# Attention and two feed-forward layers on one core: a planner's waits, row stores, read bursts, output copies and load depth

## The chip, the cores and the metric

The kernel runs on one NeuronCore of a Trainium2 chip, in one launch. The metric is device time in microseconds (us), lower is better. Five engines work side by side, each through its own instructions in order: TensorE (PE in the profile, with its weight loads as PEld), VectorE (DVE), ScalarE (ACT), GpSimd (POOL) and SyncE (SP), which issues every DMA here. They meet only in semaphores.

## The reference

Attention of 4 batches, 12 heads, 448 positions and 64 channels, with an RMS norm on queries and keys, followed by two feed-forward layers on the 1792 x 768 result:

```python
q_n, k_n = (rmsnorm(q, g_q), rmsnorm(k, g_k))
scores = scale * np.matmul(q_n, k_n.transpose(0, 1, 3, 2))
attn = softmax(scores)                       # over the last axis
x = np.matmul(attn, v)                       # to (B*S, H*D) = (1792, 768)
h = x @ w_in;  x = np.maximum(h, 0.0) ** 2 @ w_out          # d_ff 2048
g = x @ w_gate;  x = (silu(g) * (x @ w_val)) @ w_out        # d_ff 1536
```

## The kernel before, in words

**Pairs of heads.** Attention works on 24 pairs of heads, six pairs to a batch. For a pair, `all_scores` writes four groups of score tiles to PSUM (sc), `softmax` takes their maxima on VectorE and the exponentials on ScalarE into a ring of six tiles (ring), `all_transposes` turns each of the seven tiles on TensorE into a PSUM bank (pt), `turned_tile` copies it out, mostly on ScalarE, and `all_values` multiplies by v into another PSUM bank (o). `pair_outputs` multiplies o by the inverse sums (zb), which gives the rows ox; `finished_rows` stores ox to DRAM (x1d) and splits it in two parts, a rounded one and the rest, as x1. Two PSUM banks (`t_banks`) serve pt, o, small transposes (rows) and, for the first pairs, spread vectors.

**Spread vectors.** Key scales (rk) and inverse sums (zb) are needed along the other axis. For the first five pairs TensorE spreads them; from pair 5 (`SPREAD_K`, `SPREAD_Z`) they go to DRAM and are read back, broadcast, in two pieces (rkb, L646) and three pieces (zb, L808). For pairs below `SPREAD_Z` the o bank is copied out first, and is free at once; for the others it is held until zb has come.

**Fillers.** While attention runs, TensorE fills its spare time with the first six column blocks of the first layer for batches 0 to 2 (`ffn1a`: h_a and ya) and the beginning of batch 3 (`lead`: h_lead, lead2). They need the x1 of a whole batch and decoded weights.

**Sweeps.** Then `products` runs 14 sweeps: a sweep takes one batch over some column blocks f, with h products (or h_g and h_v) of 18 matmuls each, and 18 matmuls into the six PSUM banks y0 to y5 two blocks later (`BEHIND`). While a sweep runs, `load_x` fetches the six tiles xr of the next one from DRAM, casts each on ScalarE (L214) and subtracts on VectorE (L1101). `Partial` fetches earlier partial sums (yp), and `written` takes y out of PSUM and stores it. Six SBUF tiles (`io_free`) are shared by xr, yp and the copies of y. All matmuls use two-part operands, so a product takes three passes (`mm3`). The weights come in 8-byte words (raw) and are decoded by ScalarE, VectorE and GpSimd (wa, wt, hi, lo).

**Who sets the order.** The program is written by a planner in Python. Every piece of work is a generator that yields the costs of its next instruction on the engines that could run it (`{"A": 467, "V": 535}`, ns), a condition, or a number, which is a wait in planned time. `simulate` runs a clock over them; `dispatch` gives a free engine the job of the lowest rank and emits the instruction. A planned wait emits nothing: it only changes what is emitted before what. Attention has rank by pair, fillers come last. SP's jobs cost 475 ns each, and a transfer is taken to land 900 ns after its share of 300 bytes per ns.

Of the kernel before, what the change touches and what calls it, by code (L numbers as in the profile page):

```python
# [10 lines left out]
F32R = mybir.dt.float32r  # L11
# [6 lines left out]
B, H, S, D = 4, 12, 448, 64  # L18
# [33 lines left out]
BEHIND = 2  # L52
X_AT = 3
DEC_FIRST = 14
DEC_STEP = 6
# [4 lines left out]
PREP_AHEAD = 4  # L60
DMA_MARGIN = 0
A_SPARE = 600
# [12 lines left out]
def attention_two_ffn_kernel(  # L75
# [141 lines left out]

    def dma(issue, nbytes):
        yield DMA_MARGIN
        while nbytes >= DMA_BULK and dma_free[0] > clock[0] + 1100 + DMA_QUEUE:  # L220
            yield dma_free[0] - clock[0] - 1100 - DMA_QUEUE
        yield {"S": 475}, issue, nbytes

# [283 lines left out]
    def stats(b, p, n):  # L507
# [18 lines left out]
        if b * PB + p + n > SPREAD_K:  # L526
            yield from dma(lambda e: e.dma_start(out=rk_d[b][p * PT:(p + n) * PT, :], in_=rows), 0)
        rkr_free.append(where)
# [110 lines left out]
    def load_rk(g, kr):  # L639
        b, p = divmod(g, PB)  # L640
        yield lambda: rk_free and g in rows_ready
        where = rk_free.pop(0)
        rk = tile_at(where, [128, S], F32, f"rkb{g}")
        for i in range(2):
            yield from dma(
                lambda e: e.dma_start(out=rk[64 * i:64 * i + 64], in_=half(rk_d[b], 2 * p + i, 64)), 64 * S * 4  # L646
            )
        yield from prep_k(g, kr, rk, where)
# [51 lines left out]
    def probs(n):  # L700

        return ring[:, n % RING]

    def all_scores(me):
        for n in range(NH // 2 * len(GROUPS)):
# [4 lines left out]
            yield lambda: s_banks and g in qs and g in ks  # L710
            where = s_banks.pop(0)
            bank = tile_at(where, [128, 2, 512], F32, f"sc{n}")
            parts = [bank[:, t] for t in range(2)]
# [65 lines left out]
    def norms(g):  # L779
# [19 lines left out]
        yield 200  # L799
        yield from dma(lambda e: e.dma_start(out=z_d[g], in_=rows), 0)  # L800
        zr_free.append(zr_at)
# [3 lines left out]
        flat = z_d[g].rearrange("r c -> (r c)")  # L805
        for p, to, at, w in ((0, 0, 0, S), (64, 384, S, 64), (64, 0, 512, 384)):
            src = flat[bass.ds(at, w)].unsqueeze(0).to_broadcast([64, w])
            yield from dma(lambda e: e.dma_start(out=zb[p:p + 64, to:to + w], in_=src), 64 * w * 4)  # L808
        zinv[g] = zb, zb_at

    def all_transposes(me):


        for n in range(NT):
# [7 lines left out]
            ps = tile_at(where, [128, 512], F32, f"pt{n}")  # L822
            p = probs(n)

            def turn(e):
# [21 lines left out]
    def all_values(me):  # L847
        for g in range(NH // 2):
# [4 lines left out]
            o = tile_at(o_at, [128, S], F32, f"o{g}")  # L853
            v, v_at = vs.pop(g)

            def chain(e):
# [12 lines left out]
    def pair_outputs(g, o, o_at):  # L869

        yield settle["P"]
        yield lambda: ox_free and (g < SPREAD_Z or g in zinv)
        ox_at = ox_free.pop(0)
        ox = tile_at(ox_at, [128, S], F32, f"ox{g}")
        if g < SPREAD_Z:
            yield {"A": 467, "V": 535}, lambda e: copy(e, ox, o)
            t_banks.append(o_at)
            o = ox
            yield lambda: g in zinv
        zb, zb_at = zinv.pop(g)  # L880
        yield {"V": 535}, lambda e: e.tensor_tensor(out=ox, in0=o, in1=zb, op=ALU.mult)
        if g >= SPREAD_Z:
            t_banks.append(o_at)
        (zb_free if zb_at[0] is ap else t_banks).append(zb_at)
        yield from finished_rows(g, ox, ox_at)

    def finished_rows(g, ox, ox_at):
# [9 lines left out]
        def store():  # L897
            yield from dma(lambda e: e.dma_start(out=x1_d[b][j], in_=ox), 128 * S * 4)
            let_go()
# [186 lines left out]
    def x_tiles(n, second, ts):  # L1086
        def tile_of(j):
            pool = xp2 if second and j < 4 else xp
            ts.append(pool.tile([128, 2, S], F32R, tag=f"x{j + 2 if second and j >= 4 else j}", name=f"x_{n}_{j}"))
            return ts[j]  # L1090

        return tile_of

    def load_x(src, n, tiles, done):

# [11 lines left out]
        for j in range(KD):  # L1107
            yield lambda: io_free
            yield from part(j, io_free.pop(0))

# [6 lines left out]
    def products():  # L1117
# [4 lines left out]
        for i, (layer, b, fs, last_use, partial, dst) in enumerate(sweeps):  # L1122
            n = f"{layer}_{i}"
            done = None
            for f in fs:
                if f == fs[X_AT if len(fs) > 6 else 1] and i + 1 < len(sweeps):
                    nxt, done = [], []
                    src = (x1_d if sweeps[i + 1][0] == 1 else x2_d)[sweeps[i + 1][1]]
                    spawn(load_x(src, n, x_tiles(n, i % 2 == 0, nxt), done), k)
                name = f"{n}_{f}"  # L1130
# [30 lines left out]
    class Partial:  # L1161
# [6 lines left out]
        def load(self):  # L1168
            while io_free and len(self.tiles) < KD:
                j = len(self.tiles)  # L1170
                self.at[j] = io_free.pop(0)
# [19 lines left out]
    def out_of(name, n, layer, f, first, last, release_it, ys, sums, dst, k):  # L1191
# [3 lines left out]
        s, where = ready.pop(name)  # L1195
        for j in range(KD):
            if first:
                ys[j] = ps_y.tile([128, S], F32, tag=f"y{j}", name=f"y_{n}_{j}")
            yield from mm3(ys[j], w[0], w[1], bass.ts(j, 128), s[:, 0, :], s[:, 1, :], first, last)
            if last:  # L1200
                spawn(written(ys[j], sums, j, n, dst[j]), k - 2)
# [87 lines left out]
```

## Time and profile before

| | us |
|---|---|
| median of 3 runs (1318.31 to 1320.59) | 1318.47 |
| the profiled execution's own time | 1317.27 |
| its span, first to last instruction | 1315.5 |
| PE busy in the span | 1279.3 (97%) |
| PEld busy | 1082.3 (82%) |
| DVE, ACT, POOL busy | 671.0, 568.4, 153.3 |

An engine's busy time is the union of its instructions. A matmul's end is modelled, so two neighbours overlap in the list; what a product costs is read from the starts. Idle time before an instruction stands in brackets with its releaser, the event that came last. The granted clock of TensorE is a share of full speed: 1.00 is 2.4 GHz and 0.50 is 1.2 GHz. A row name like `y<-s,hi_out` is the tile written and the tiles read.

### The profile page before, as it was taken

Reading aid. Unit: us, or ns where it says so; the run is one execution under the profiler, and the core shown is the slowest. Engines: PE = TensorE matmul, PEld = TensorE weight load, DVE = VectorE, ACT = ScalarE, POOL = GpSimd, SP = SyncE. Lnnn points to the kernel's source line nnn. Section 1 sums busy time; section 2 is a strip of 40 time slices with the busy share of each in tenths; the row PEclk is TensorE's granted clock in tenths of the full one; section 3 lists DMA queues with packets and bytes.
Section 4 is the critical chain, followed back from the end, with each engine's and each line's share of the span. In section 5 each row is a group of like instructions: output and inputs, shape, how many; then the busy total and the mean of one; then the engine's idle time right before and its main releaser. Section 6 shows DMA issues by size and latency. Waiting matters only on the chain.

```text
span 1315.5 us, 18513 instructions
## 1 busy us (share of the span) xinstructions
PE 1279.3 (97%) x6709; PEld 1082.3 (82%) x6709; DVE 671.0 (51%) x1366; ACT 568.4 (43%) x1251; POOL 153.3 (12%) x256
## 2 busy tenths in 40 slices
PE   8887999999999999999999989999999999999998
PEld 6554666667678899999999979999999999999998
DVE  7898965653433996248634675121238911213122
ACT  6897867875763655225422352121215511211110
POOL 4454343333201000000000000000000000000000
PEclk9999999999999999999999989999999999999999
DMA  6566554432212664246434454020116500303021
GB/s 207 170 203 194 166 162 148 143 109 77 92 38 75 220 200 162 81 132 207 154 113 127 143 189 153 1 84 1 63 37 207 174 0 1 105 0 118 10 84 42
DMA packets 85469, 151.02 MB, mean 115 GB/s; under 512 B 14641, under 2 KB 64962, under 8 KB 85378
## 3 DMA queue, kind: packets, MB, share of 16 engines
q1 hardware_dynamic: 85378, 149.84, 36.2%
q8 instruction: 53, 0.87, 0.3%
q14 instruction: 38, 0.31, 0.1%
HBM read 120.75 MB, written 29.04 MB: 114 GB/s over the span
## 4 chain that ended last, share of the span: by engine, by line
PE 70%; DVE 2%; DMA 1%; ACT 1%; issue 0%; SPq 0%; DVEq 0%; ACTq 0%
PE y L321 26%; PE h_v L321 14%; PE h_g L321 13%; PE h L321 12%; PE h_a L321 2%; PE ya L321 1%; PE o L859 1%; PE pt L827 1%; DMA xr<-x2d 1%; PE sc L722 1%; DMA raw_in<-in_w_in_dram 0%; DVE lo_out L308 0%; DVE wt_out L290 0%; DVE wt_out L293 0%; DVE wt_in L290 0%
## 5 line engine op out<-in xcount | busy, mean ns | idle before, releaser
L321 PE MATMUL h_g<-x,hi_g 128*128 128x448 f32 x576 | 165.5, 368 | 5.7 <-ACT x L214 5.5
L321 PE MATMUL h_v<-x,hi_v 128*128 128x448 f32 x576 | 165.4, 368 | 0.0
L321 PE MATMUL y<-s,hi_o 128*128 128x448 f32 x576 | 164.1, 366 | 0.0
L321 PE MATMUL y<-s,hi_out 128*128 128x448 f32 x552 | 158.7, 369 | 2.5 <-DVE r L358 2.3
L321 PE MATMUL h<-x,hi_in 128*128 128x448 f32 x516 | 147.7, 367 | 0.0
L764 ACT ACTIVATE ring<-sc,m,rms 128x448 f32<-128x448 f32 x168 | 122.8, 732 | 53.6 <-PE pt L827 46.2
L374 DVE TENSOR_TENSOR sig<-h_g,sig 128x448 f32<-128x448 f32 x48 | 29.9, 624 | 212.9 <-ACT sig L373 212.9
L321 PEld LDWEIGHTS h_g<-x,hi_g 128*128 128x128 f32 x576 | 108.4, 188 | 16.3 <-ACT x L214 6.3
L373 ACT ACTIVATE sig<-h_g 128x448 f32<-128x448 f32 x48 | 26.1, 545 | 218.8 <-PE h_g L321 218.7
L750 DVE TENSOR_REDUCE sc<-sc 128x1 f32<-128x448 f32 (+1 forms) x96 | 93.9, 978 | 50.9 <-PE sc L722 41.1
L321 PEld LDWEIGHTS h_v<-x,hi_v 128*128 128x128 f32 x576 | 109.0, 189 | 9.5
L321 PEld LDWEIGHTS y<-s,hi_o 128*128 128x128 f32 x576 | 108.1, 188 | 9.3
L827 PEld LDWEIGHTS pt<-ident,ring 128*128 128x128 f32 x672 | 73.7, 142 | 50.3 <-ACT turned_p L214 11.6
L321 PEld LDWEIGHTS y<-s,hi_out 128*128 128x128 f32 x552 | 104.4, 189 | 12.0 <-DVE r L358 2.7
L827 PE MATMUL pt<-ident,ring 128*128 128x128 f32 x672 | 102.7, 283 | 6.9 <-ACT ring L764 3.0
L321 PE MATMUL h_v<-x,lo_v 128*128 128x448 f32 x288 | 105.8, 367 | 0.0
L321 PE MATMUL h_g<-x,lo_g 128*128 128x448 f32 x288 | 105.6, 367 | 0.0
L321 PE MATMUL y<-s,lo_o 128*128 128x448 f32 x288 | 105.4, 366 | 0.0
L321 PEld LDWEIGHTS h<-x,hi_in 128*128 128x128 f32 x516 | 96.9, 188 | 9.1 <-DVE x L1101 0.7
L321 PE MATMUL y<-s,lo_out 128*128 128x448 f32 x276 | 101.3, 367 | 0.0
L214 ACT COPY turned_p<-pt 128x512 f32<-128x512 f32 x163 | 93.8, 588 | 4.9 <-PE pt L827 4.7
L321 PE MATMUL h<-x,lo_in 128*128 128x448 f32 x258 | 94.4, 366 | 0.0
(154 smaller groups left out, 2139.0 us busy)
## 6 DMA issues: line engine op xcount, KB each, us to landing
raw_in<-in_w_in_dram SPq DMA_DIRECT2D x32, 384.0 KB
raw_out<-in_w_out_dram SPq DMA_DIRECT2D x32, 384.0 KB
kq<-in_kq_p_dram SPq DMA_DIRECT2D x23, 480.0 KB
xr<-x2d SPq DMA_DIRECT2D x42, 224.0 KB
raw_g<-in_w_gate_dram SPq DMA_DIRECT2D x24, 384.0 KB
raw_v<-in_w_val_dram SPq DMA_DIRECT2D x24, 384.0 KB
raw_o<-in_w_out_dram SPq DMA_DIRECT2D x24, 384.0 KB
xr<-x1d SPq DMA_DIRECT2D x36, 224.0 KB
```

The costliest lines, as they stand in the source:

```text
L214: e.copy(out, src)
L321: return {"P": 203}, lambda e: e.matmul(ps, lhsT=w, rhs=x, start=first, stop=last), 0
L373: yield {"A": 424}, lambda e: e.activation(out=t, in_=pg, func=ACTF.Sigmoid)
L374: yield {"V": 535}, lambda e: e.tensor_tensor(out=t, in0=pg, in1=t, op=ALU.mult)
L722: e.matmul(parts[t][:, :S], lhsT=q[a][d, bass.ts(i % 4, 128)], rhs=k[c][d], start=(p == 0), stop=(p == len(passes) - 1),)
L750: e.tensor_reduce(out=top, in_=sc, axis=AX.X, op=ALU.max, negate=True)
L764: yield {"A": 704}, lambda e: e.activation(out=probs(at + t), in_=parts[t][:, :S], func=ACTF.Exp, bias=m[:, t:t + 1], scale=rq[:, i:i + 1] ...
L827: e.transpose(ps[:, bass.ts(j, 128)], p[:, bass.ds(min(128 * j, S - 128), 128)], ident)
L859: e.matmul(o[64 * h:64 * h + 64], lhsT=v[:, 4 * h + j], rhs=turned_p[:, 2 * j + h], start=(j == 0), stop=(j == 3),)
```

## The change

Six edits:

1. Each of the spread reads (two pieces of rkb, three of zb) is issued as one planned job, so that no other DMA stands between its pieces, and the planner adds 1500 ns (`ROUND_TRIP`) to the landing of these reads and of the writes before them.
2. A row store of x1 is offered to SP 2500 ns later (`STORE_HOLD`).
3. The o bank of pairs 5 to 13 is now copied out too (`EVACUATE` = 14): nine more copies, and nine multiplications that read SBUF in place of PSUM.
4. From the time that batch 0's x1 is complete until the fillers are all planned, scores, transposes and value products are offered to TensorE 500 ns later (`PE_SLACK`, `linger`).
5. `load_x` keeps three tiles in flight in place of one (`X_FLIGHT`).
6. The six output products of a block, and the loads of partial sums, go in the order 2, 3, 4, 5, 0, 1 (`OUT_ORDER`).

```diff
+X_FLIGHT = 3
+PE_SLACK = 500
+OUT_ORDER = [2, 3, 4, 5, 0, 1]
...
-DMA_MARGIN = 0
+STORE_HOLD = 2500
+ROUND_TRIP = 1500
+EVACUATE = 14
...
-    def dma(issue, nbytes):
-        yield DMA_MARGIN
+    def dma(issue, nbytes, hold=0, landing=0, n=1):
+        yield hold
         while nbytes >= DMA_BULK and dma_free[0] > clock[0] + 1100 + DMA_QUEUE:
             yield dma_free[0] - clock[0] - 1100 - DMA_QUEUE
-        yield {"S": 475}, issue, nbytes
+        yield {"S": 475 * n}, issue, nbytes
+        yield landing
...
-        for i in range(2):
-            yield from dma(
-                lambda e: e.dma_start(out=rk[64 * i:64 * i + 64], in_=half(rk_d[b], 2 * p + i, 64)), 64 * S * 4
-            )
+
+        def read(e):
+            for i in range(2):
+                e.dma_start(out=rk[64 * i:64 * i + 64], in_=half(rk_d[b], 2 * p + i, 64))
+
+        yield from dma(read, 128 * S * 4, landing=ROUND_TRIP, n=2)
...
+    def linger():
+        if KD - 1 in x1[0] and not filled:
+            yield PE_SLACK
...
             where = s_banks.pop(0)
+            yield from linger()
...
-        for p, to, at, w in ((0, 0, 0, S), (64, 384, S, 64), (64, 0, 512, 384)):
-            src = flat[bass.ds(at, w)].unsqueeze(0).to_broadcast([64, w])
-            yield from dma(lambda e: e.dma_start(out=zb[p:p + 64, to:to + w], in_=src), 64 * w * 4)
+
+        def read(e):
+            for p, to, at, w in ((0, 0, 0, S), (64, 384, S, 64), (64, 0, 512, 384)):
+                src = flat[bass.ds(at, w)].unsqueeze(0).to_broadcast([64, w])
+                e.dma_start(out=zb[p:p + 64, to:to + w], in_=src)
+
+        yield from dma(read, 128 * S * 4, landing=ROUND_TRIP, n=3)
...
             p = probs(n)
+            yield from linger()
...
             v, v_at = vs.pop(g)
+            yield from linger()
...
-        yield lambda: ox_free and (g < SPREAD_Z or g in zinv)
+        yield lambda: ox_free and (g < EVACUATE or g in zinv)
...
-        if g < SPREAD_Z:
+        if g < EVACUATE:
             yield {"A": 467, "V": 535}, lambda e: copy(e, ox, o)
             t_banks.append(o_at)
...
-            yield from dma(lambda e: e.dma_start(out=x1_d[b][j], in_=ox), 128 * S * 4)
+            yield from dma(lambda e: e.dma_start(out=x1_d[b][j], in_=ox), 128 * S * 4, hold=STORE_HOLD)
...
         for j in range(KD):
-            yield lambda: io_free
-            yield from part(j, io_free.pop(0))
+            yield lambda: io_free and j - len(done) < X_FLIGHT
+            spawn(part(j, io_free.pop(0)), rank)
...
-                j = len(self.tiles)
+                j = OUT_ORDER[len(self.tiles)]
...
-        for j in range(KD):
-            if first:
+        if first:
+            for j in range(KD):
                 ys[j] = ps_y.tile([128, S], F32, tag=f"y{j}", name=f"y_{n}_{j}")
+        for j in OUT_ORDER:
             yield from mm3(ys[j], w[0], w[1], bass.ts(j, 128), s[:, 0, :], s[:, 1, :], first, last)
```

Where the instructions now stand is shown at three places. The first is TensorE just after the value product of pair 5 (o5); pt43 and pt44 are transposes of pair 6, sc29 is a score group of pair 7, h_a0 is filler. Before:

```order
L827 MATMUL pt42_1638<-ident_205,ring_266 128x128 x4
L722 MATMUL sc28_1617<-kst7_1439,qst7_1437 128x448
L722 MATMUL sc28_1617<-kst_lo7_1440,qst7_1437 128x448
L722 MATMUL sc28_1617<-kst7_1439,qst_lo7_1438 128x448
L321 MATMUL h_a0_1_1337<-x1_2_1101,lo_in1_822 128x448
L321 MATMUL h_a0_0_1336<-x1_3_1287,hi_in0_667 128x448
L722 MATMUL sc29_1659<-kst7_1439,qst7_1437 128x448 x2
```

And now:

```order
L845 MATMUL pt42_1640<-ident_205,ring_266 128x128 x4
L735 MATMUL sc28_1614<-kst7_1439,qst7_1437 128x448
L735 MATMUL sc28_1614<-kst_lo7_1440,qst7_1437 128x448
L735 MATMUL sc28_1614<-kst7_1439,qst_lo7_1438 128x448
L327 MATMUL h_a0_1_1337<-x1_2_1101,lo_in1_822 128x448
L845 MATMUL pt43_1659<-ident_205,ring_266 128x128 x4
L845 MATMUL pt44_1669<-ident_205,ring_266 128x128 x4
L327 MATMUL h_a0_0_1336<-x1_3_1288,hi_in0_667 128x448 x2
L327 MATMUL h_a0_0_1336<-x1_3_1288,lo_in0_668 128x448
L327 MATMUL h_a0_1_1337<-x1_3_1288,hi_in1_821 128x448
L735 MATMUL sc29_1683<-kst7_1439,qst7_1437 128x448 x2
```

Two transposes and four filler matmuls now stand ahead of sc29, where one filler matmul stood. From o7 on the number of fillers ahead of a value product differs: 486 filler matmuls stood ahead of the end of the last one (o23) before, and 559 of the 702 do now. The number of TensorE's matmuls of every kind is the same in both.

The second place is SP's queue in the last sweep of the first layer (xr_1_6 are the tiles that the first sweep of the second layer reads). Before:

```order
L1098 DMA xr_1_6_0_7998<-x2d2_0_93 128x448
L271 DMA raw_o24_0_8010<-in_w_out2_dram 128x768
L271 DMA raw_o24_1_8013<-in_w_out2_dram 128x768
L271 DMA raw_g5_0_8048<-in_w_gate_dram 128x768
L1098 DMA xr_1_6_1_8068<-x2d2_1_94 128x448
L271 DMA raw_g5_1_8086<-in_w_gate_dram 128x768
L271 DMA raw_v5_0_8109<-in_w_val_dram 128x768
L1098 DMA xr_1_6_2_8130<-x2d2_2_95 128x448
L271 DMA raw_v5_1_8145<-in_w_val_dram 128x768
L271 DMA raw_o25_0_8149<-in_w_out2_dram 128x768
L271 DMA raw_o25_1_8173<-in_w_out2_dram 128x768
L1098 DMA xr_1_6_3_8179<-x2d2_3_96 128x448
```

And now:

```order
L1117 DMA xr_1_6_0_8008<-x2d2_0_93 128x448
L1117 DMA xr_1_6_1_8014<-x2d2_1_94 128x448
L1117 DMA xr_1_6_2_8025<-x2d2_2_95 128x448
L277 DMA raw_o24_0_8021<-in_w_out2_dram 128x768
L277 DMA raw_o24_1_8024<-in_w_out2_dram 128x768
L1117 DMA xr_1_6_3_8081<-x2d2_3_96 128x448
L277 DMA raw_g5_0_8065<-in_w_gate_dram 128x768
L1117 DMA xr_1_6_4_8097<-x2d2_4_97 128x448
L1117 DMA xr_1_6_5_8104<-x2d2_5_98 128x448
L277 DMA raw_g5_1_8119<-in_w_gate_dram 128x768
```

Between the first and the sixth xr tile stood eleven weight reads and five reads of partial sums; now three weight reads stand there.

The third place is TensorE at the first output product of the sweeps (s_1_0_0 comes from the fillers' h_lead0). Before it began with y_1_0_0 and y_1_0_1:

```order
L321 MATMUL y_1_0_0_5336<-s_1_0_0_5262,hi_out0_1626 128x448 x2
L321 MATMUL y_1_0_0_5336<-s_1_0_0_5262,lo_out0_1627 128x448
L321 MATMUL y_1_0_1_5345<-s_1_0_0_5262,hi_out0_1626 128x448 x2
L321 MATMUL y_1_0_1_5345<-s_1_0_0_5262,lo_out0_1627 128x448
L321 MATMUL y_1_0_2_5354<-s_1_0_0_5262,hi_out0_1626 128x448 x2
```

Now it begins with y_1_0_2, and its last three products are:

```order
L327 MATMUL y_1_0_5_5356<-s_1_0_0_5275,hi_out0_1624 128x448 x2
L327 MATMUL y_1_0_5_5356<-s_1_0_0_5275,lo_out0_1625 128x448
L327 MATMUL y_1_0_0_5351<-s_1_0_0_5275,hi_out0_1624 128x448 x2
L327 MATMUL y_1_0_0_5351<-s_1_0_0_5275,lo_out0_1625 128x448
L327 MATMUL y_1_0_1_5352<-s_1_0_0_5275,hi_out0_1624 128x448 x2
L327 MATMUL y_1_0_1_5352<-s_1_0_0_5275,lo_out0_1625 128x448
```

The four products into y2 to y5, of three matmuls each, moved ahead of those into y0 and y1.

## Rows read from the trace of the kernel before

**Rows 1.** The page's busy time, share of the span and instructions, of two engines.

```profile
PE 1279.3 (97%) x6709; PEld 1082.3 (82%) x6709; DVE 671.0 (51%) x1366; ACT 568.4 (43%) x1251; POOL 153.3 (12%) x256
```

**Rows 2.** Windows by stage: length, busy PE, PEld, DVE, ACT, POOL; PEclk, DMA share, GB/s.

```profile
104.00:135.00 31.00, 23.99 (x127) 15.69 (x126) 25.65 (x52) 22.57 (x54) 13.36 (x21) 0.89 0.65 189
135.00:204.00 69.00, 63.58 (x369) 42.66 (x367) 53.06 (x103) 51.98 (x125) 28.46 (x43) 0.98 0.53 162
204.00:440.00 236.00, 235.46 (x1351) 169.79 (x1348) 115.06 (x225) 153.91 (x363) 59.10 (x91) 1.00 0.34 104
440.00:452.00 12.00, 9.45 (x38) 8.01 (x37) 11.95 (x28) 8.01 (x18) 0.00 (x0) 0.86 0.54 175
452.00:764.00 312.00, 311.98 (x1531) 286.90 (x1530) 182.76 (x379) 121.55 (x244) 2.05 (x2) 1.00 0.48 151
764.00:782.00 18.00, 12.27 (x47) 9.98 (x46) 12.81 (x29) 9.63 (x18) 0.00 (x0) 0.81 0.71 234
782.00:1315.50 533.50, 529.75 (x2598) 487.36 (x2596) 178.30 (x338) 112.89 (x221) 1.09 (x1) 1.00 0.20 67
```

**Rows 3.** Waits of PE from 104 to 204 us: total, times, longest, us.

```profile
PE sc L722 <- ACT ring L764: 6.1, 6, 1.8
PE pt L827 <- DVE ox L881: 2.6, 1, 2.6
PE rows L600 <- POOL lo_out L308: 1.4, 1, 1.4
PE h_a L321 <- DVE r_a L358: 1.2, 1, 1.2
PE pt L827 <- ACT turned_p L214: 0.8, 1, 0.8
```

**Rows 4.** Windows of the four stretches at half clock after 104 us.

```profile
125.60:132.40 6.80, 5.57 (x19) 3.84 (x20) 3.80 (x8) 3.00 (x8) 0.93 (x1) 0.50 0.56 171
200.70:204.10 3.40, 3.40 (x16) 2.09 (x13) 2.65 (x6) 2.88 (x8) 1.34 (x2) 0.50 0.28 92
446.40:449.80 3.40, 3.40 (x9) 3.06 (x10) 3.40 (x9) 2.02 (x4) 0.00 (x0) 0.50 0.59 217
774.10:780.90 6.80, 4.43 (x11) 3.67 (x12) 2.85 (x6) 4.10 (x7) 0.00 (x0) 0.50 0.63 206
```

**Rows 5.** Timeline of PE, 430 to 470 us: start, length, operation, count, [idle <-releaser].

```profile
446.40 1.11 PE L321 MATMUL y<-s,hi_out 128*128 128x448 f32 x2 [2.34 <-DVE r L358]
...
447.68 0.95 PE L321 MATMUL y<-s,hi_out 128*128 128x448 f32 x2
448.43 0.57 PE L321 MATMUL y<-s,lo_out 128*128 128x448 f32 x1
...
454.75 0.57 PE L321 MATMUL y<-s,hi_out 128*128 128x448 f32 x2
455.16 0.36 PE L321 MATMUL y<-s,lo_out 128*128 128x448 f32 x1
```

**Rows 6.** Timeline of PE, 763 to 790 us.

```profile
770.97 0.47 PE L321 MATMUL h_g<-x,hi_g 128*128 128x448 f32 x1 [1.36 <-ACT x L214]
...
776.47 1.40 PE L321 MATMUL h_g<-x,hi_g 128*128 128x448 f32 x2 [4.18 <-ACT x L214]
```

**Rows 7.** Timeline of DVE, 443 to 448 us.

```profile
445.73 0.61 DVE L358 SCALAR_TENSOR_TENSOR r<-lead,r 128x448 f32<-128x448 f32 x1
```

**Rows 8.** Timeline of SP's queue, 745 to 778 us: the first and the sixth read.

```profile
746.72 0.40 SPq L1098 DMA_DIRECT2D xr<-x2d  x1
...
771.60 0.32 SPq L1098 DMA_DIRECT2D xr<-x2d  x1
```

**Rows 9.** Waits of ACT from 104 to 204 us.

```profile
ACT wa_out L276 <- DMA raw_out<-in_w_out_dram: 5.4, 2, 3.2
```

**Rows 10.** The tile xr: duration min/median/max in ns, first and last start, form.

```profile
L1101 DVE TENSOR_TENSOR x<-xr,x x78: 605/619/629, 457.3 to 1214.9; 128x448 fp32r<-128x448 f32 x78
```

**Rows 11.** Groups by shape, 0 to 135 us: busy, mean ns, idle before.

```profile
L214 ACT COPY ox<-o 128x448 f32<-128x448 f32 x5 | 2.7, 530 | 0.5 <-PE o L859 0.5
```

More of the change, by code (lines that the diff above doesn't have):

```diff
@@ L526, in stats @@
         if b * PB + p + n > SPREAD_K:
-            yield from dma(lambda e: e.dma_start(out=rk_d[b][p * PT:(p + n) * PT, :], in_=rows), 0)
+            yield from dma(lambda e: e.dma_start(out=rk_d[b][p * PT:(p + n) * PT, :], in_=rows), 0, landing=ROUND_TRIP)
         rkr_free.append(where)
@@ L799, in norms @@
         yield 200
-        yield from dma(lambda e: e.dma_start(out=z_d[g], in_=rows), 0)
+        yield from dma(lambda e: e.dma_start(out=z_d[g], in_=rows), 0, landing=ROUND_TRIP)
         zr_free.append(zr_at)
@@ L881, in pair_outputs @@
         yield {"V": 535}, lambda e: e.tensor_tensor(out=ox, in0=o, in1=zb, op=ALU.mult)
-        if g >= SPREAD_Z:
+        if g >= EVACUATE:
             t_banks.append(o_at)
@@ L1088, in tile_of, with load_x @@
             pool = xp2 if second and j < 4 else xp
-            ts.append(pool.tile([128, 2, S], F32R, tag=f"x{j + 2 if second and j >= 4 else j}", name=f"x_{n}_{j}"))
+            ts[j] = pool.tile([128, 2, S], F32R, tag=f"x{j + 2 if second and j >= 4 else j}", name=f"x_{n}_{j}")
             return ts[j]
         return tile_of
-    def load_x(src, n, tiles, done):
+    def load_x(src, n, tiles, done, rank):
         def part(j, where):
@@ L1126, in products @@
                 if f == fs[X_AT if len(fs) > 6 else 1] and i + 1 < len(sweeps):
-                    nxt, done = [], []
+                    nxt, done = {}, []
                     src = (x1_d if sweeps[i + 1][0] == 1 else x2_d)[sweeps[i + 1][1]]
-                    spawn(load_x(src, n, x_tiles(n, i % 2 == 0, nxt), done), k)
+                    spawn(load_x(src, n, x_tiles(n, i % 2 == 0, nxt), done, k), k)
                 name = f"{n}_{f}"
```

## The prediction

> **What bounds the kernel now.** I read the page's busy times first, then windows by stage, then TensorE's waits in the stages where it stood still, and last the timelines around the long waits. The reader is to see four things.
>
> TensorE is busy 97% of the span, and no other engine is above 51% [rows 1]. The number of its matmuls stays the same, and so does each one's work; so the time can only move by TensorE's idle time and by its clock.
>
> By stage [rows 2], 204 to 440, 452 to 764 and 782 to the end lose almost nothing: 0.5 us, 0.02 us and 3.75 us, the last being the tail after the final matmul, which nothing here touches. Before 104 us the order of TensorE is unchanged by the edits, so that part keeps its gaps. Three stages are left: **A**, 104 to 204 us, busy 23.99 + 63.58 = 87.6 of 100, idle 12.4; **B**, 440 to 452, idle 2.55; **C**, 764 to 782, idle 5.73.
>
> The waits name the causes. In A they come to 12.1 us: six score groups behind an exponential 6.1, one transpose behind the multiplication by zb 2.6, and three small kinds 3.4 [rows 3]. In B it is one wait of 2.34 us for VectorE's reading of the bank lead2 [rows 5]. In C a gate product waits 1.36 and 4.18 us for its x tiles [rows 6].
>
> After such waits the clock falls. Four stretches ran at 0.50, which is 1.2 GHz [rows 4], each just after the engine had stood idle (2.58 us ahead of 200.7 is the 2.6 of rows 3; 2.34; 4.18). At half clock two matmuls start 0.75 us apart, from 447.68 to 448.43, and at full clock 0.41, from 454.75 to 455.16 [rows 5]. So half of the busy time in a stretch is lost: 5.57/2 = 2.8 and 3.40/2 = 1.7 in A, 3.40/2 = 1.7 in B, 4.43/2 = 2.2 in C.
>
> The most that can be won is thus 12.4 + 4.5 = 16.9 in A, 4.25 in B, 7.9 in C: 29.
>
> **C: three x tiles in flight, 7.9 us.** Before, a tile was fetched, cast and subtracted before the next was asked for. The six reads went out from 746.72 to 771.60 [rows 8], five pitches of 4.98 us, of which the subtraction alone is 0.62 [rows 10]. The sixth tile came 5.7 us too late. Now the order has the six in two rounds with three weight reads between. The first still cannot go out before 746.72, since the six shared tiles are held until then by the sums of the sweep before. Two rounds at 4.98 end at 757; at twice that, at 767. The sixth tile is wanted at about 770, since the wait that 776.47 ends began at 772.3. So the stall goes, with a margin of some 5 us in the bad case and 15 in the good one, and the 2.2 of slow clock with it. The weight reads that now stand behind the x tiles are late by a few us, but the block that they feed is some 50 us away.
>
> **B: the order of output products, 4.0 us.** The wait for lead2's bank began at 446.40 - 2.34 = 444.06, on the product into y1. Now four products of three matmuls, at 0.203 each 2.4 us, stand ahead of it that stood behind. It is wanted at 446.5, and VectorE leaves the bank at 445.73 + 0.61 = 446.34 [rows 7], and stands in the same place of its queue. 2.3 us of the 2.55 go, and 1.7 of clock. What is late next is y0, which waits only for TensorE's own earlier writes.
>
> **A: attention offered later, nine copies more, 10.7 us.** A planned wait emits no instruction, so the 500 ns cost the chip nothing in themselves; they let fillers stand ahead of a product. I take the waits one by one.
>
> The 2.6 us are a transpose that had no bank, since o was held until zb had landed. Pairs 5 to 13 now copy o out, and this pair is among them: all of it goes, and the 1.7 of clock behind it.
>
> Of the 6.1, in six waits, the longest is 1.8. There, at sc29, TensorE now has eight transposes of 0.1 and four filler matmuls of 0.2 ahead where it had one matmul: 1.6 us for 0.2. Elsewhere I count the planned 0.5 us each. I leave 2.3 of the 6.1.
>
> The waits of `rows` (1.4) and of the filler h_a (1.2) are not offered later by any edit; I leave 2.0 of 2.6. Of the 0.8 behind a copied transpose I leave 0.2, and 0.3 that no wait explains stays. Left 4.8, won 7.6. The slow stretch at 125.6 follows just these waits of `rows` and h_a, so I take half of its 2.8: 1.4. With the 1.7 this is 10.7. Unknown is how exactly the plan meets the chip; the bounds are 0, the same waits elsewhere, and 16.9.
>
> **What the edits add.** Nine copies of 0.53 us on ScalarE, where five made it wait 0.5 us in all [rows 11], come to 9 x 0.63 = 5.7 us. ScalarE is busy 22.57 + 51.98 = 74.6 of the 100 us of A [rows 2], and TensorE has fillers to run meanwhile, so I cost them at nothing; if the fillers were short, at 5.7. The nine multiplications are the same work from another memory. The row stores are only offered later: one of the two ox tiles is held 2.5 us longer, against some 15 us from pair to pair. The reads back to back add no DMA; on SP, whatever would have stood between two pieces now goes behind the last, by 0.5 or 1 us. Nothing in A's waits names a row store or value load, so this is nothing too. The last value product now has 559 filler matmuls ahead and not 486; the 143 behind it are 29 us of work, which covers the last pair's way to x1.
>
> **The sum.** 10.7 + 4.0 + 7.9 = 22.6 us off the profiled execution's 1317.27 gives 1294.7. The median of the runs, 1318.47, lies 1.2 above that execution, so I predict 1295.9 us.
>
> **Rivals.**
>
> *Weights hold ScalarE.* In A ScalarE waited 5.4 us in two waits for raw weights to land, 3.2 the longest [rows 9], with exponentials queued behind. The planner counts 300 bytes per ns, and 189 and 162 GB/s were moved in A [rows 2]. No edit mends that: waits of 1 to 3 us against an offset of 0.5 would come back at other places. Then A gives nothing, and the time is 1295.9 + 10.7 = 1306.6. Against it: the planner put more than 0.5 us ahead at the worst place. 0.12.
>
> *Three transfers share what one had.* If the DMA engines are the limit, three tiles in flight take three times as long, C's stall stays, and the time is 1295.9 + 7.9 = 1303.8. For it: the engines were busy 0.71 of 764 to 782. Against: 0.48 over the sweeps before [rows 2], and a pitch that contains waits on two other engines. The Trainium skill states this mechanism (DMA: Bandwidth & Descriptors, Rules for kernel authors): two transfers use the same 16 DMA engines, so that splitting work between them brings no bandwidth. The trace agrees only so far as those shares show room: the 0.48 and 0.71 leave some. 0.05.
>
> *The shared tiles run out: slower.* The six tiles also take y out of PSUM, in the five sweeps without partial sums to add. With three of them filled by x tiles, a copy of y would wait for one to be landed, cast and subtracted, up to a pitch of 4.98 us, and TensorE with it, since the next sweep wants the y bank; with a slow stretch of 1.7 behind, 6.7 us a place. From the fourth place on (22.6/6.7 = 3.4) the change loses; at all five it is 1295.9 + 33.5 = 1329.4. For it: nothing waited so before, when one tile was in flight. Against: TensorE lost 0.02 us in the 312 us with the first such place [rows 2], three tiles are left for y, and between a bank's last product and its next lie at least 18 matmuls, 3.7 us. 0.07.
>
> **How the numbers follow.** The forecast has 0.70. The remaining 0.06 are for small mixtures, half of them without a measurable effect. The range goes from A won in full, 6.2 better, to the first rival: 1289 to 1307; it leaves out the slower rival and the stray cases, under 2 in 10. About 0.2%, 2.6 us, is what a measurement of this kernel can tell from no change. Faster: 0.70 + 0.12 + 0.05 + 0.03 = 0.90; within: 0.03; slower: 0.07.
>
> **What would show it.** C right: no wait of a gate product for x at the start of the second layer, the clock at 1.00 there, and six reads of xr within some 14 us. B right: no wait of y for lead's reader, and no slow stretch after it. A right: TensorE idle about 5 us in 104 to 204, no transpose waiting for ox; wrong, if the waits of score groups still come to 6 us. The prediction as a whole is wrong if waits of y for copies appear at sweep changes, or idle time in 204 to 440.

## The result, and the profile after

The changed kernel takes 1301.86 us (median of 4 runs, 1299.92 to 1302.11) where the kernel before, on the same chip, takes 1319.53: a ratio of 0.9856, with a 95% interval of 0.9827 to 0.9884. It is faster, as forecast; the forecast time, 1295.9, was 6.0 us too low. The profiled execution took 1302.11, its span 1300.3.

The page's busy times of the changed kernel answer to [rows 1]:

```profile
PE 1275.2 (98%) x6709; PEld 1081.4 (83%) x6709; DVE 665.5 (51%) x1359; ACT 574.5 (44%) x1267; POOL 152.3 (12%) x257
```

As many matmuls as before. ScalarE has 6.1 us more and VectorE 5.5 less. The nine copies, 0.53 us each, are 4.8; but a run with five copies, shown below, has 575.3 on ScalarE too, so some other work has moved from VectorE to ScalarE. The windows by stage of the changed kernel have the columns of [rows 2] (length, busy PE, PEld, DVE, ACT, POOL; PEclk, DMA share, GB/s):

```profile
57.90:104.00 46.10, 40.26 (x268) 25.04 (x269) 41.99 (x92) 39.69 (x99) 21.56 (x28) 0.93 0.56 172
104.00:135.00 31.00, 26.48 (x151) 16.81 (x150) 28.14 (x59) 27.36 (x68) 12.83 (x20) 0.96 0.63 194
135.00:204.00 69.00, 67.29 (x397) 46.46 (x397) 51.71 (x105) 58.52 (x141) 29.37 (x46) 0.99 0.58 177
204.00:440.00 236.00, 233.92 (x1349) 170.50 (x1347) 114.84 (x227) 157.17 (x374) 58.36 (x92) 1.00 0.35 108
440.00:452.00 12.00, 10.48 (x52) 9.73 (x53) 12.00 (x28) 6.70 (x14) 0.00 (x0) 1.00 0.64 184
452.00:764.00 312.00, 312.00 (x1533) 287.44 (x1532) 186.45 (x386) 125.04 (x249) 2.05 (x2) 1.00 0.49 155
764.00:782.00 18.00, 18.00 (x90) 16.51 (x89) 12.99 (x29) 8.56 (x17) 0.00 (x0) 1.00 0.53 181
```

Against [rows 2], 104 to 204 us now loses 6.2 us and not 12.4, the output products from 440 lose 1.5 and stay at full clock, and from 764 nothing is lost: 18.00 of 18 busy at 1.00, where it was 12.27 at 0.81. So far the forecast. But the windows of two kernels hold different work at the same hour, and the first row, from 57.9 to 104, has a clock of 0.93 in a part that the forecast called unchanged.

So I cut both traces at the same work, not the same time: at the first matmul of the value products of the third and of the sixth pair (tile o), at the first output product (y), at the first matmul into h after it, and at the end. TensorE's work is nearly the same between two such marks, whichever kernel it is. In us, before and changed, from two profiles of each:

| stretch | before | changed |
|---|---|---|
| start to third pair's o | 57.4, 60.8 | 60.2, 57.9 |
| third to sixth pair's o | 42.3, 41.7 | 46.4, 46.4 |
| sixth pair's o to y (holds A) | 343.1, 345.6 | 332.9, 334.3 |
| y to h (B) | 8.3, 6.2 | 5.6, 5.1 |
| h to the end (holds C) | 864.4, 864.9 | 855.3, 855.3 |

In the means A gave 10.8 us, B 1.9, C 9.4; and 4.4 was lost between the third and the sixth pair, where nothing was forecast to move. The start varies by 2 to 3 us in either kernel.

Where A's waits stood in [rows 3], the changed kernel has these (waits of PE from 104 to 204 us: total, times, longest):

```profile
PE h_a L327 <- DVE r_a L364: 3.2, 1, 3.2
PE pt L845 <- ACT ox L219: 1.3, 2, 1.0
PE rows L606 <- ACT turned_p L219: 1.3, 1, 1.3
PE sc L735 <- ACT ring L777: 0.4, 1, 0.4
```

The six waits of score groups (6.1) shrank to one of 0.4, and the transpose behind the multiplication by zb (2.6) is gone. The filler h_a waits longer than before, 3.2 for 1.2, and transposes now wait for the new copies of o.

The reads of x ahead of C, in the timeline of SP's queue, answer to [rows 8]:

```profile
740.22 1.38 SPq L1117 DMA_DIRECT2D xr<-x2d  x3
...
742.60 0.42 SPq L1117 DMA_DIRECT2D xr<-x2d  x1
...
744.16 1.38 SPq L1117 DMA_DIRECT2D xr<-x2d  x2
```

All six are out within 5.3 us, by 745.54, where the first and the sixth stood 24.9 us apart. A tile is ready for TensorE when it is cast and subtracted; VectorE's subtractions of the last two, and the window of the reads (columns as above):

```profile
752.29 1.15 DVE L1120 TENSOR_TENSOR x<-xr,x 128x448 fp32r<-128x448 f32 x2
```

```profile
740.00:746.00 6.00, 6.00 (x31) 5.57 (x30) 5.92 (x14) 2.97 (x7) 0.00 (x0) 1.00 0.92 288
```

The sixth tile is ready at 753.44, 13.2 us after the first read went out; in the kernel before it was ready at 777.08, 30.4 us after. The DMA engines are busy 0.92 while the reads go out.

### The profile page after: what moved, and what is told of

Same layout as the page of the kernel before. It is cut to its first block, busy times and chain, and to the rows that moved or that the text cites. A ratio compares the mean times of both kernels' runs of the same rounds, so it can differ in the third digit from the quotient of the medians.

```text
span 1300.3 us, 18510 instructions
## 1 busy us (share of the span) xinstructions
PE 1275.2 (98%) x6709; PEld 1081.4 (83%) x6709; DVE 665.5 (51%) x1359; ACT 574.5 (44%) x1267; POOL 152.3 (12%) x257
## 4 chain that ended last, share of the span: by engine, by line
PE 85%; DVE 6%; ACT 3%; DMA 2%; issue 2%; POOL 1%; SPq 0%; DVEq 0%; POOLq 0%; ACTq 0%
PE y L327 26%; PE h_v L327 14%; PE h_g L327 14%; PE h L327 12%; PE o L878 4%; PE ya L327 4%; PE pt L845 3%; PE sc L735 3%; PE h_a L327 3%; DVE sc L763 1%; ACT ring L777 1%; ACT turned_p L219 1%; DMA nat<-in_q_n_dram 1%; DMA nat<-in_k_n_dram 1%; DVE wt_in L299 0%
## 5 line engine op out<-in xcount | busy, mean ns | idle before, releaser
L327 PEld LDWEIGHTS y<-s,hi_out 128*128 128x128 f32 x552 | 103.6, 188 | 10.7 <-DVE s L368 1.9
L845 PEld LDWEIGHTS pt<-ident,ring 128*128 128x128 f32 x672 | 77.8, 141 | 33.2 <-issue 7.6
```

What stands on the lines that cost most here:

```text
L327: return {"P": 203}, lambda e: e.matmul(ps, lhsT=w, rhs=x, start=first, stop=last), 0
L845: e.transpose(ps[:, bass.ts(j, 128)], p[:, bass.ds(min(128 * j, S - 128), 128)], ident)
```

## The experiments

Each run is the changed kernel with the edit shown, timed beside the kernel before; all ratios are against that. For the changed kernel I take 1301.4 us, the mean of its two medians.

**Both kernels again.** No edit; it asks whether the beginning differs by chance.

> The changed kernel once more, unchanged, for its profile. Its first value product of pair 5 began at 106.5 us, against 99.7 before, though TensorE's list up to there is the same. Theory (chance of the execution): it begins anywhere from 99 to 107 us here, with 7 to 20 us at half clock ahead of it. Rival (something in the changed program slows its beginning): it begins at 106 to 107 us again.

> The kernel before once more, for its profile. Theory (chance of the execution): the value product of pair 5 begins anywhere from 99 to 107 us. Rival: at 99 to 101 us again. The stalls in A, B and C are to come back in their places in either case: 12 us idle from pair 5 to pair 12, 2.3 us at the first y, 5.7 us at the first h_g.

Measured: changed 1300.98 us, ratio 0.9865 (0.9848 to 0.9881); before 1320.36, ratio 1.0015 (0.9995 to 1.0034). The table above has their stretches. The start up to the third pair's o is chance: each kernel has a good and a bad one. The 46.4 against 42 behind it is not: it came again to a tenth.

**One x tile in flight.**

```diff
-X_FLIGHT = 3
+X_FLIGHT = 1
```

> The changed kernel with one x tile in flight again. Theory: C's stall of 5.7 us and its slow stretch of 2.2 come back whole, 7.9 us slower than the changed kernel (about 1309.8 us), with the waits of h_g for x near the start of the second layer. Rival (transfers share what one had): nothing changes there, since the tiles would land no earlier with three in flight; then the time stays at 1301.9 and the stall was cured by another edit.

Measured: 1311.22 us, ratio 0.995 (0.9933 to 0.9967). Its waits of PE from 760 to 790 us, and its window of C:

```profile
PE h_g L327 <- ACT x L219: 5.7, 2, 4.3
```

```profile
764.00:782.00 18.00, 12.10 (x43) 9.54 (x42) 10.72 (x23) 7.61 (x14) 0.00 (x0) 0.72 0.64 211
```

[Rows 6] are back, slow clock and all. Three tiles in flight are worth 1311.2 - 1301.4 = 9.8 us by the medians, and 865.3 - 855.3 = 10.0 by the stretch from h to the end.

**The old order of output products.**

```diff
-OUT_ORDER = [2, 3, 4, 5, 0, 1]
+OUT_ORDER = [0, 1, 2, 3, 4, 5]
```

> The changed kernel with the output products in the order 0 to 5 again. Theory: the wait of y for the reader of lead2's bank comes back, 2.3 us, with a slow stretch of 1.7: some 2.5 to 4 us slower than the changed kernel, less what now waits there anyway (1.6 us for s, which would overlap). Rival: the wait for s (1.6 us in the changed kernel) hides the bank's wait, so that the order is worth under 1 us.

Measured: 1305.41 us, ratio 0.9899 (0.9885 to 0.9914), 4.0 us above the changed kernel. The timeline of PE, 436 to 456 us:

```profile
442.12 0.47 PE L327 MATMUL y<-s,hi_out 128*128 128x448 f32 x1 [1.19 <-DVE s L368]
...
444.67 0.69 PE L327 MATMUL y<-s,hi_out 128*128 128x448 f32 x2 [1.87 <-DVE r L364]
```

The second wait, for VectorE's reading of lead2's bank, is that of [rows 5]; it is absent in the changed kernel. The first one, for s, is there in both (1.60 in the changed kernel).

**All DMA edits undone.** Reads in pieces as before, no hold on stores, no planned round trip; the generators of rkb and zb are those of the kernel before.

```diff
-STORE_HOLD = 2500
-ROUND_TRIP = 1500
+STORE_HOLD = 0
+ROUND_TRIP = 0
...
-        yield from dma(read, 128 * S * 4, landing=ROUND_TRIP, n=2)
+        for i in range(2):
+            yield from dma(
+                lambda e: e.dma_start(out=rk[64 * i:64 * i + 64], in_=half(rk_d[b], 2 * p + i, 64)), 64 * S * 4
+            )
```

> The changed kernel with its first two edits taken back: reads of a spread row in two or three pieces with other reads between, no hold on row stores, no planned round trip. The four other edits stay. Theory 'the order of the reads slows the beginning': SP's queue is now as before up to the end of the first 50 us and further, so from the third to the sixth value product TensorE takes 42 us as before (41.7 and 42.3) and not the 46.3 to 47.3 of the four runs with the new order; no wait of rows for a sum of about 2 us and no half-clock stretch at 70 to 75 us. The time falls from the changed kernel's 1301.4 by 4 to 5 us to about 1297, ratio about 0.983, unless waits of score groups come back between 104 and 204 us, by 1 to 2 us. Rival 'chance, or something else in the program': 46 to 47 us stay, and the time stays at 1301 (0.987).

Measured: 1297.18 us, ratio 0.9822 (0.9793 to 0.9852), and 41.9 us from the third to the sixth pair. So edits 1 and 2 cost 4 to 5 us there, though the orders of the four other engines are the same with and without them from the start to past the place shown below. Which of the two?

**No planned round trip; no held stores.** Two runs, each with one line:

```diff
-ROUND_TRIP = 1500
+ROUND_TRIP = 0
```

> The changed kernel with the planned round trip of 1500 ns set to 0; reads back to back and the hold on row stores stay. In SP's queue the two reads of the sixth pair's spread row go back ahead of the nat read that they stand behind in the changed kernel; the row store stays one place later. Theory 'the spread reads pushed behind nat start VectorE's and POOL's squares on top of each other': the third to sixth value product take about 42 us and the total is 1297 (0.983). Rival 'the later row store, or the pieces being back to back, does it': 46 to 47 us stay and the time is 1301 (0.987).

```diff
-STORE_HOLD = 2500
+STORE_HOLD = 0
```

> The changed kernel with STORE_HOLD = 0 and nothing else: the row store of the fourth pair goes back in SP's queue right behind the spread row's store, ahead of the two nat reads that it stands behind in the changed kernel; the reads stay back to back and the round trip stays planned. Theory 'the held store lets nat in early, and GpSimd's squares then run beside VectorE's work': VectorE's kst_lo of the sixth pair takes 0.61 us as in the kernel before and not 1.35, rows waits about 0.6 us for its sum and not 2.05, no half-clock stretch at 70 to 75 us, 42 us from the third to the sixth value product and not 46.3 to 47.7, and the time falls by some 5 us to 1297 (0.982). Rival 'the pieces back to back do it': 1.35, 2.05 and 47 us stay, and the time stays at 1301.5 (0.986).

Measured: without the round trip 1302.01 us, ratio 0.9847 (0.982 to 0.9874), 47.7 us from the third to the sixth pair: my theory of the pushed-back reads fell. Without the hold 1297.94, ratio 0.9821 (0.9797 to 0.9844), and 42.3 us. It is the held store, and the timelines show how. First the changed kernel, 65.4 to 73.2 us, all engines (SPq is SP's queue):

```profile
65.84 0.37 SPq L533 DMA_DIRECT2D rkd<-rkr  x1
66.26 0.36 SPq L492 DMA_DIRECT2D nat<-in_k_n_dram  x1
...
67.25 0.58 SPq L492 DMA_DIRECT2D nat<-in_q_n_dram  x1
67.92 0.38 SPq L917 DMA_DIRECT2D x1d<-ox  x1
...
69.67 1.25 POOL L495 TENSOR_TENSOR nat<-nat 128x448 f32<-128x448 f32 x1
70.05 1.35 DVE L663 TENSOR_TENSOR kst_lo<-kq,kst 128x448 fp32r<-128x448 f32 x1
71.38 1.08 POOL L495 TENSOR_TENSOR nat<-nat 128x448 f32<-128x448 f32 x1 [0.46 <-DMA nat<-in_q_n_dram]
...
71.60 0.89 DVE L796 TENSOR_SCALAR sum<-sum 128x7 f32<-128x7 f32 x1
...
72.87 0.30 PE L606 MATMUL rows<-ident,sum 128*128 128x128 f32 x1 [2.06 <-DVE sum L797]
```

Then the same work without the hold, 62.6 to 69 us:

```profile
63.06 0.37 SPq L533 DMA_DIRECT2D rkd<-rkr  x1
63.53 0.34 SPq L917 DMA_DIRECT2D x1d<-ox  x1
...
64.50 0.58 SPq L492 DMA_DIRECT2D nat<-in_k_n_dram  x1
65.13 0.42 SPq L492 DMA_DIRECT2D nat<-in_q_n_dram  x1
...
67.27 0.61 DVE L663 TENSOR_TENSOR kst_lo<-kq,kst 128x448 fp32r<-128x448 f32 x1
...
68.08 0.16 DVE L796 TENSOR_SCALAR sum<-sum 128x7 f32<-128x7 f32 x1
...
68.60 1.08 POOL L495 TENSOR_TENSOR nat<-nat 128x448 f32<-128x448 f32 x1 [1.67 <-DMA nat<-in_k_n_dram]
68.61 0.30 PE L606 MATMUL rows<-ident,sum 128*128 128x128 f32 x1 [0.57 <-DVE sum L797]
```

Read them from the store rkd on. With the hold, the row store x1d comes late and nat's first read 0.42 us after rkd; without it the store and a read of v go first, and nat 1.44 after (0.87 in the kernel before, where only the store stands between). So with the hold nat lands while GpSimd is still at other work: its square of nat starts at once, at 69.67, and runs beside VectorE's kst_lo. Without it GpSimd stands idle 1.67 us for nat, and kst_lo is over before it starts. Beside the square, kst_lo takes 1.35 us and not 0.61; beside the second square the little scaling of sum takes 0.89 and not 0.16. These two delays of 0.73 + 0.74 are what TensorE's wait for the sums grew by, 2.06 - 0.57 = 1.49. In the other six profiles with the hold the second delay falls one operation earlier, on the cast between kst_lo and the scaling, which takes 1.08 us for 0.35, and the scaling takes 0.16; the wait is 2.04 to 2.06 in all seven. So in the second profile of the changed kernel:

```profile
68.97 1.08 DVE L221 CAST hi_in<-wt_in 128x384 fp32r<-128x384 f32 x1
69.97 0.16 DVE L796 TENSOR_SCALAR sum<-sum 128x7 f32<-128x7 f32 x1
```

Then the clock falls; the window of that slow clock in the changed kernel, and the windows from the third to the sixth pair's o, first of the changed kernel and then without the hold:

```profile
74.30:81.10 6.80, 6.80 (x32) 3.28 (x32) 5.74 (x13) 4.71 (x13) 0.00 (x0) 0.50 0.50 154
```

```profile
60.15:106.50 46.35, 40.51 (x259) 24.87 (x255) 42.28 (x93) 39.94 (x100) 20.70 (x28) 0.93 0.57 174
```

```profile
57.42:99.71 42.29, 37.23 (x259) 23.54 (x255) 41.00 (x93) 39.84 (x99) 20.44 (x28) 1.00 0.64 191
```

The same 259 matmuls are busy 40.5 us for 37.2, which is the slow clock (half of 6.80 us, 3.4), and TensorE is idle 5.8 us for 5.1: the wait grew by 1.5, and other waits shrank by some 0.7. So most of the loss is the clock. The Trainium skill has a rule for such pairs (SBUF — State Buffer, SBUF: two separate sides): VectorE and GpSimd share one pair of SBUF ports, and when a VectorE operation with two SBUF inputs meets a GpSimd one that reads SBUF, or is in a mode that uses both ports, whichever starts first keeps the pair for its whole instruction while the other stands still. The rows fit it: kst_lo, which has two SBUF inputs, ends 0.48 us after its square, and by the rule would end its own 0.61 after; the scaling of sum ends at 72.49, 0.03 after the square beside it, and by the rule 0.16 after; both are 0.13 short. Whether the scaling and the cast, with one input each, run in such a mode no run here shows, and that the port is the means was not tried apart. That the hold brings the overlap is what the two runs show; that the overlap brings the slow clock is argued from its place in all seven profiles, since no run has the overlap without the hold.

**No slack; five copies.** Two runs for edits 4 and 3:

```diff
-PE_SLACK = 500
+PE_SLACK = 0
```

> The changed kernel with PE_SLACK = 0: score groups, transposes and value products are offered as soon as planned ready, and 473 instead of 559 filler matmuls stand ahead of the last value product. Theory of the prediction: of the 12.1 us of waits between the sixth and the thirteenth value product before (6 now) the waits of score groups come back, 3 to 5 us, with a half-clock stretch of 1.7 to 2.8: 1301.4 + 5 = 1306.5 (0.990). Rival 'the copied-out o alone does it; the slack is only an order': stage stays near 119 us and the time at 1301 (0.987).

```diff
-EVACUATE = 14
+EVACUATE = 5
```

> The changed kernel with EVACUATE = 5: as before, only the first five pairs' o are copied out at once. Theory of the prediction: a transpose waits again for a bank that a pair's o holds until its reciprocal row has landed, 2 to 3 us at one or two places between the sixth pair and 204 us, with 1.7 us at half clock behind: 1301.4 + 4.3 = 1305.7 (0.990). Rival 'the copies cost ScalarE as much as they free': the same time, 1301 (0.987), with the waits of transposes for ox (0.7, 0.96 and 0.4 us in the changed kernel) gone in return.

Measured: without slack 1302.55 us, ratio 0.9864 (0.984 to 0.9889), not to be told from the changed kernel by its time; the sixth pair's o to y takes 336.4 for 332.9 and 334.3, some 3 us more. The waits of score groups, which the theory saw come back, are 0.6 us in 104 to 204. With five copies 1294.09, ratio 0.9802 (0.9777 to 0.9827): 7.3 us faster than with fourteen, against both theories. Of it 5 us lie between the sixth pair's o and h, 333.6 for 338.5 and 339.4; the rest is within what two executions differ by. The waits of PE from 104 to 204 us with five copies:

```profile
PE sc L735 <- ACT ring L777: 1.0, 1, 1.0
PE h_a L327 <- DVE r_a L364: 0.9, 1, 0.9
...
PE pt L845 <- DVE ox L900: 0.5, 1, 0.5
```

The wait that the copies were to remove is there, at 0.5 us and not 2.6, and h_a waits 0.9 for 3.2. The copies' own cost is in the groups by shape from 0 to 204 us (busy, mean ns | idle before and why), first of the changed kernel and then with five copies:

```profile
L219 ACT COPY ox<-o 128x448 f32<-128x448 f32 x11 | 5.8, 526 | 6.7 <-PE o L878 6.6
```

```profile
L219 ACT COPY ox<-o 128x448 f32<-128x448 f32 x5 | 2.6, 529 | 3.5 <-PE o L878 3.4
```

Besides their 3.2 us of work, six more copies make ScalarE stand 3.2 us longer with its queue behind them, until o is done. That this is what TensorE loses is not shown, and the wait of h_a has another cause in sight. Ahead of it VectorE is late, by operations that stretch beside GpSimd as kst_lo did: two subtractions lo_out together, where the run with five copies has one that is over in 0.71:

```profile
125.28 2.85 DVE L314 TENSOR_TENSOR lo_out<-wt_out,hi_out 128x384 fp32r<-128x384 f32 x2
```

```profile
117.18 0.71 DVE L314 TENSOR_TENSOR lo_out<-wt_out,hi_out 128x384 fp32r<-128x384 f32 x1
```

In the second profile of the changed kernel it is one lo_out of 1.63 us and a multiplication ox that now reads o's copy:

```profile
124.81 1.35 DVE L900 TENSOR_TENSOR ox<-ox,zb 128x448 f32<-128x448 f32 x1
```

**What ends A's waits.** With the DMA order of before, two more runs, each on top of the DMA diff above: slack without the copies (EVACUATE = 5), and copies without the slack (PE_SLACK = 0).

> The DMA edits undone as in the run before and EVACUATE = 5 as well: left of the change are PE_SLACK = 500, X_FLIGHT = 3 and OUT_ORDER. Theory 'the two costs are apart in time and add': the third to sixth value product 42 us; from the sixth to the first output product about 334 us as with EVACUATE = 5 alone (351.4 and 351.8 before, 338.5 and 339.4 in the changed kernel); time 1301.4 - 4.3 - 7.3 = 1290 (0.977), which beats both kernels. Rival 'the copied-out o or the new order of reads is what ended the waits of the middle stage': without both that part returns towards 350 us and the time is 1303 or above (0.988).

> The DMA edits undone and PE_SLACK = 0: left are EVACUATE = 14, X_FLIGHT = 3 and OUT_ORDER. Theory 'the slack ends the waits of the middle stage and the copies only cost': from the sixth value product to the first output product about 351 + 4 us as before the change, time about 1297 + 16 = 1313 (0.995). Rival 'each of the two is enough by itself, since either one redraws a plan that happened to be unlucky': about 340 us there, as with PE_SLACK = 0 alone (342.1), and a time of 1298 to 1300 (0.984).

Measured: slack alone 1296.23 us, ratio 0.9815 (0.979 to 0.984); copies alone 1304.54, ratio 0.9865 (0.9837 to 0.9892). The stretch from the sixth pair's o to h, which is A and B:

| | no copies | copies |
|---|---|---|
| no slack | 351.4, 351.8 (kernel before) | 341.7 |
| slack | 337.2 | 336.5 |

The three changed cells have the new output order too, which is 2 to 4 us of each. With the reads of before, the slack by itself ends nearly all of A, and the copies add 0.7 to it. The copies by themselves end some 6 to 8 us, and the slack adds 5.2 to them, 7.4 by the medians (1304.54 for 1297.18). So neither expectation held whole. The costs did not add up to 1290, since with these reads the copies cost next to nothing. And of the rival 'each of the two is enough' the stretch of about 340 us fits, but not the time of 1298 to 1300. Five copies without the slack, with the reads back to back, were not run. In the run with slack and no copies a long wait for ox as in [rows 3] is still there, behind the ninth pair and not the eleventh; its timeline, 150 to 168 us:

```profile
154.67 0.55 SPq L819 DMA_DIRECT2D zb<-zd  x1
...
157.57 0.45 SPq L819 DMA_DIRECT2D zb<-zd  x1
...
159.83 0.45 SPq L819 DMA_DIRECT2D zb<-zd  x1
...
167.00 0.62 DVE L894 TENSOR_TENSOR ox<-o,zb 128x448 f32<-128x448 f32 x1 [0.51 <-DMA zb<-zd]
...
167.68 0.55 PE L839 MATMUL pt<-ident,ring 128*128 128x128 f32 x3 [2.14 <-DVE ox L894]
```

Three reads for one zb, spread over 5.6 us between other transfers, and a transpose waits 2.14 us. With reads back to back, and five copies, that wait is 0.5; in the run below, which differs from this one by edit 1 alone, the longest is 0.7. So edit 1 does without ScalarE what the copies were to do. Its two parts, the reads back to back and the planned round trip, were not tried apart with five copies.

**The best of it: no hold, five copies.**

```diff
-STORE_HOLD = 2500
+STORE_HOLD = 0
...
-EVACUATE = 14
+EVACUATE = 5
```

> The changed kernel with STORE_HOLD = 0 and EVACUATE = 5: the reads back to back, the planned round trip, the slack, three x tiles and the new output order stay. If the store's hold is what slows the beginning and the nine copies what slows the middle, both are gone here: 42 us from the third to the sixth value product, about 334 from the sixth to the first output product, and 1290 (0.977). If the pieces back to back slow the beginning, 47 us stay and the time is 1294 (0.980) as with EVACUATE = 5 alone.

Measured: 1292.46 us (4 runs, 1290.32 to 1294.73), ratio 0.9786 (0.9761 to 0.9811), 9 us below the changed kernel and faster than both kernels; from the run with five copies and the hold (1294.09) it can't be told by its time. Its page and its windows of A:

```profile
PE 1274.1 (99%) x6709; PEld 1081.3 (84%) x6709; DVE 664.3 (51%) x1357; ACT 573.8 (44%) x1265; POOL 149.6 (12%) x255
```

```profile
104.00:135.00 31.00, 27.86 (x164) 18.20 (x163) 27.70 (x60) 28.04 (x67) 13.49 (x21) 1.00 0.69 211
135.00:204.00 69.00, 67.12 (x396) 45.71 (x394) 53.13 (x105) 58.07 (x141) 28.82 (x52) 1.00 0.59 176
```

A runs at full clock throughout. From the sixth pair's o to h it takes 333.1 us, the least of all runs; kst_lo is at 0.62. From the third to the sixth pair it took 44.4 with 6.8 us at half clock from 84.5 on, whose cause stays open; the wait for the sums is 0.59 there. So of the expectation the 42 us did not come, while 333.1 and 1292.5 are near its 334 and 1290.

Whether the store is held sorts all fourteen profiles:

| | kst_lo, us | third to sixth pair, us |
|---|---|---|
| held: changed (2), X_FLIGHT = 1, old OUT_ORDER, ROUND_TRIP = 0, PE_SLACK = 0, EVACUATE = 5 | 1.35 in all seven | 46.2 to 47.7 |
| not held: before (2), DMA undone, and with five copies, and without slack, STORE_HOLD = 0 | 0.61 to 0.62 | 41.7 to 42.3 |
| not held: STORE_HOLD = 0 with five copies | 0.62 | 44.4 |

## Why the prediction was right, and where it was not

The forecast was faster by 22.6 us; it is faster by 17.7. The sign and the three stages were right, one part of the sum was missing.

**The step that failed** is the sentence "Before 104 us the order of TensorE is unchanged by the edits, so that part keeps its gaps", with its companion that the row stores "are only offered later". Up to the place of the loss, near 70 us, the orders of four engines are indeed unchanged. But SP's is not, and I asked only what a held store is late for, not what goes ahead in its place. It was nat: its first read follows the store rkd by 0.42 us for 0.87, and GpSimd's square of it starts 0.38 us ahead of kst_lo and not 0.80 behind it, beside VectorE's work. That cost 4.4 us, in the stretch that I had left out of the sum. Without the hold the kernel takes 1297.9, and the forecast was 1295.9.

**C, 7.9 forecast:** 9.8 by the run with one tile, so the stall and its slow clock are gone, and 2 us more than I had counted, part of it slow clock: its profile has 0.72 in that window where [rows 2] have 0.81; the rest stays open. The sixth tile was ready 13.2 us after the first read, between my bounds of 10 and 20.

**B, 4.0 forecast:** 4.0 by the run with the old order. In the profiles it is 1.9, since a wait for s, 0.2 us in the first profile of the kernel before, is 1.6 and 1.2 in the changed one. The slow stretch that I counted at 1.7 is not there each time: the second profile of the kernel before has the wait, 2.28 us, and full clock behind it.

**A, 10.7 forecast:** 10.8 by the profiles, but not by the steps that I added up; that the two agree is luck. I left 2.3 of the score waits, and 0.4 stayed. I let the copies take the 2.6 behind zb; they do, but so do reads back to back. I laid the slow stretch at 125.6 to the waits of rows and h_a, but h_a's ended at 127.15, inside it. And I costed the nine copies at nothing, with 5.7 as the bound if the fillers were short: with the new reads they cost 5 us, and 3.5 without the hold (336.6 to 333.1). With the old reads they are worth 0.7 (337.2 to 336.5), no more than chance. The h_a wait, of which I left the old size, grew to 3.2 with fourteen copies; it is 2.2 to 3.2 in seven of the nine profiles with fourteen copies and absent in two, and 0.9 or absent in the three with five copies and the slack. Nor are the nine multiplications "the same work from another memory": the 185 that read o from PSUM in the fourteen profiles took 0.61 to 0.63 us each, and of the 81 that the nine more copies moved to SBUF eleven took 0.86 to 1.70, each beside a GpSimd operation.

**The rivals.** The weights did not hold ScalarE: A gave its gain. Three transfers did not take three times as long, but they did take longer: from read to cast the first tile took 3.7 us and the sixth 7.1, where one in flight took 3.6 to 4.7, and the share of the DMA engines was 0.92 while the reads went out, against 0.82 from the first to the sixth read in the kernel before. So far the trace agrees with the rule of the Trainium skill that I had named beside this rival (DMA: Bandwidth & Descriptors, Rules for kernel authors), that transfers share the same 16 engines; it did not keep the six tiles from being ready in 13.2 us for 30.4. The shared tiles did not run out: 452 to 764 us is busy 312.00 of 312.00. One mark of a failure appeared in small: 204 to 440 us lost 2.1 us and not 0.5, in waits of 0.2 to 0.6 us.

## What to carry to other kernels

When a transfer is held back in a queue, list what moves ahead of it and which engines that starts earlier: an engine off the critical path can hurt by being early, here GpSimd beside VectorE. When two edits aim at one wait, time each without the other: here the copies and the reads back to back both cut the wait for zb, and with both in place the copies only had a price. Compare traces at the same work and not at the same time, or a loss in one stage reads as a gain that came late.

## What was not expected of the hardware

A short VectorE operation can be stretched several times by a GpSimd one beside it: 128x7 elements took 0.89 us for 0.16, 128x448 from two operands 1.35 for 0.61, and a cast of 128x384 took 1.08 for 0.35 in six profiles. So one engine can hold up another with no semaphore between them, beyond what the beginning of this document says of how they meet. The multiplication by zb with o in PSUM was never stretched: 185 times, 32 of them beside GpSimd work. And from the start to the second pair's o, where no engine's order differs yet between the kernels, the fourteen profiles took from 45.0 to 47.9 us; to the third pair's o, from 57.2 to 61.5, with 0 to 13.7 us of it at half clock. A difference of that size between two single profiles says nothing.
